# Loading the state of two batches first, and transposing the rest by DMA, in an attention and gated feed-forward kernel

## The chip, the cores and the metric

The kernel runs on one core of one Trainium2 chip. The metric is the device time of one execution in microseconds (us). TensorE does the products, ScalarE (ACT), VectorE (DVE) and GpSimd (POOL) the elementwise work, and the core has 16 DMA engines. Loads that GpSimd issues go through the "software" queue (q0 in the profile), loads and transposes that SyncE (SP) issues through the "hardware" queue (q1). Each run also records the clock granted to TensorE, as a share of full speed.

## The reference, cut to what matters

There are 8 batches, each with x (8 heads, 512 tokens, 64 wide) and a state (8 heads, 32 slots, 64 wide). Tokens attend to slots, slots attend to tokens, and everything goes through a gated feed-forward layer.

```python
scores = x @ state^T / 8;   xread = softmax(scores) @ state     # tokens read the state
scores2 = state @ x^T / 8;  sread = softmax(scores2) @ x        # slots read the tokens
y = concat(xread, sread)                                        # 4352 rows of 512
out = (sigmoid(y @ w_gate) * (y @ w_val)) @ w_out               # d_ff = 1536
```

## The kernel before

The kernel never forms xread. It multiplies the transposed state with the gate and value weights once per batch (SW, "gate states"), and the gate products are then the transposed attention weights (aT) times SW. Each batch so needs its x and its state transposed (xT, sTc) before its scores, and aT before its gate products. The first two batches are a hand-ordered list of steps (the "head"). The other batches are prepared one ahead, between the products of the batch before.

In the head, the whole state is loaded first, then x of batch 0 and 1 and the first 256 of the 1536 columns of the weights in f32, all on the hardware queue. TensorE transposes the whole state:

```python
sf = wp.tile((128, 16, D), FP, name="sf")
nc.sync.dma_start(sf, state.rearrange("b h (u l) d -> (b h u) l d", l=16))   # 4 KB a partition
load_x(0, nc.sync, 2)
...
for i in range(2):
    ps = p_gv.tile((128, 8, 64), FP, name="stp", tag="gv")
    for l in range(8):
        for e in range(2):
            nc.tensor.matmul(ps[e * 64:(e + 1) * 64, l], sb[:, 8 * i + l], ident_e[:, e], start=True, stop=True)
```

Later in the head, GpSimd issues the last weights, x of batch 2, w_out in three parts and x of batch 3. It then casts x of batch 2, and SP transposes it by DMA, four instructions a batch:

```python
load_x(2, nc.gpsimd)
load_wo(0); load_wo(1); load_wo(2)          # w_out
load_x(3, nc.gpsimd)
...
cast_x(2, pool, 0, 4); cast_x(2, pool, 4, 4)
cast_x(3, pool, 0, 4); cast_x(3, pool, 4, 4)
at_xT_dma(2); at_xT_dma(3)
```

After the head come the output products of batch 0 (12 groups of four), and between them the attention of batch 2 and its gate states:

```python
if b == 1 and f == 1:                       # after the second group of output products
    for i in range(2):
        S_mm(nb, i, (AT, OU)[i])            # scores of batch 2: TensorE, in order
        S_exp(nb, i); n_sum(nb, i); n_mul(nb, i, nc.vector)
    aT_dma(nb)                              # its attention weights, transposed by DMA
```

In the traces of this case an engine takes its instructions in program order, and what waits at the front holds up what stands behind it: in the changed kernel GpSimd stood for 15.0 us in front of one cast, with ready work behind it.

The softmax here doesn't subtract the row's maximum and nothing guards it: scores larger than these inputs give would overflow.

## Time and profile before

| | before |
|---|---|
| device time, median of the first 4 runs | 229.31 us (229.16 to 229.48) |
| profiled span, granted clock | 227.5 us, 1.0 |
| TensorE busy | 215.7 us (95%) |
| first output product of batch 0 starts | 44.89 us |
| scores of batch 2 start | 46.62 us |

The span is shorter than the device time, since it starts at the first instruction. TensorE is full from about 20 us to the end. The lines of the profile are in the prediction below.

### The profile page before, as it was taken

The numbers are of one execution on the slowest core, as the hardware profiler recorded it, in microseconds if no ns is written. First come the engines' busy times: TensorE is split into PE (matmuls) and PEld (weight loads), VectorE is DVE, ScalarE is ACT, GpSimd is POOL, SyncE is SP. The second block draws the span as 40 slices with busy tenths as digits, with TensorE's granted clock in tenths as the row PEclk, the third lists the DMA queues.
The fourth block names the chain that finished last, engine by engine and source line by source line (L and its number), as shares of the span: only waits on it lengthen the run. The fifth ranks groups of instructions, "written<-read, shape, count | busy, mean of one in ns | idle before, by whom it ended". The sixth has DMA issues, their size and how long they took to land.

```text
span 227.5 us, 4735 instructions
## 1 busy us (share of the span) xinstructions
PE 215.7 (95%) x1831; PEld 111.6 (49%) x1856; DVE 141.4 (62%) x234; ACT 131.0 (58%) x246; POOL 44.4 (20%) x78
## 2 busy tenths in 40 slices
PE   7568999999999999999999999999999999999994
PEld 7453345444454545444544454454445444466743
DVE  2599889967448855886488638874687433422301
ACT  3677877647476566746675666656755444423311
POOL 1499930060033001500060006000200000000001
PEclk9999999999999999999999999999999999999999
DMA  6999999943699252725282431243122111111113
GB/s 213 354 176 191 233 264 242 152 80 69 145 287 248 41 132 101 231 46 124 87 252 43 83 116 46 81 83 116 46 72 69 48 46 49 67 73 46 49 35 104
DMA packets 37990, 28.09 MB, mean 123 GB/s; under 512 B 20976, under 2 KB 33136, under 8 KB 37968
## 3 DMA queue, kind: packets, MB, share of 16 engines
q1 hardware_dynamic: 32464, 21.31, 35.3%
q0 software_dynamic: 5360, 6.42, 14.8%
q8 instruction: 14, 0.23, 0.4%
q14 instruction: 8, 0.07, 0.2%
q10 hardware_dynamic: 144, 0.07, 0.1%
HBM read 18.35 MB, written 8.91 MB: 120 GB/s over the span
## 4 chain that ended last, share of the span: by engine, by line
PE 76%; DMA 11%; POOL 5%; SPq 3%; issue 2%; ACT 1%; DVE 0%; POOLq 0%; ACTq 0%
PE outp L321 35%; PE gvp L290 28%; DMA xf<-in_x_dram 8%; PE gvp L293 5%; PE swp L238 4%; DMA xT<-xb 3%; SPq L128 2%; PE srp L215 1%; POOL Eb L145 1%; PE Sp L134 1%; PE outp L341 1%; POOL wg L83 1%; POOL ab L175 1%; POOL xb L103 1%; POOL wv L94 1%
## 5 line engine op out<-in xcount | busy, mean ns | idle before, releaser
L305 DVE SCALAR_TENSOR_TENSOR glu<-th,gvp 128x512 bf16<-128x512 f32 (+1 forms) x108 | 70.2, 657 | 63.9 <-ACT th L300 48.2
L300 ACT ACTIVATE th<-gvp 128x512 f32<-128x512 f32 (+1 forms) x108 | 61.6, 575 | 62.5 <-PE gvp L290 51.2
L290 PE MATMUL gvp<-aT,SW 128*128 128x512 bf16 x384 | 96.3, 379 | 0.2
L321 PE MATMUL outp<-wo,glu 128*128 128x512 bf16 x371 | 95.1, 379 | 1.3 <-issue 0.2
L290 PEld LDWEIGHTS <-SW 128*128 128x128 bf16 x384 | 36.2, 98 | 45.1 <-issue 4.2
L321 PEld LDWEIGHTS <-glu 128*128 128x128 bf16 x396 | 37.4, 98 | 40.7 <-issue 0.4
L276 ACT CAST SW<-swp 128x512 bf16<-128x512 f32 (+1 forms) x78 | 42.2, 582 | 4.2 <-PE swp L238 2.9
L145 POOL CAST Eb<-E 128x256 bf16<-128x256 f32 x32 | 12.4, 429 | 96.2 <-ACT E L139 96.2
L325 ACT ACTIVATE res<-outp 128x512 f32<-128x512 f32 x33 | 19.7, 598 | 17.1 <-PE outp L321 17.1
L103 POOL CAST xb<-xf 128x1024 bf16<-128x1024 f32 (+1 forms) x13 | 14.6, 1147 | 20.8 <-DMA xf<-in_x_dram 20.8
L276 DVE CAST SW<-swp 128x512 bf16<-128x512 f32 x20 | 13.4, 683 | 0.7 <-PE swp L238 0.7
L175 DVE TENSOR_TENSOR ab<-E,ri 128x512 bf16<-128x512 f32 x14 | 13.7, 980 | 0.1
L332 POOL DMA_DIRECT2D out_dram<-res x2 | 1.0, 526 | 60.1 <-ACT res L325 60.1
L160 DVE TENSOR_REDUCE E<-E 128x128 f32<-128x512 f32 x12 | 12.3, 1033 | 0.0
L152 DVE TENSOR_REDUCE rs<-E 128x16 f32<-128x512 f32 x16 | 10.8, 678 | 2.0 <-ACT E L139 2.0
L238 PE MATMUL swp<-wg,sTc 64*32 64x256 bf16 (+1 forms) x256 | 11.6, 328 | 0.3
L238 PEld LDWEIGHTS <-sTc 64*32 64x32 bf16 x512 | 6.4, 90 | 10.7 <-issue 7.9
L139 ACT ACTIVATE E<-Sp 128x512 f32<-128x512 f32 x16 | 9.6, 608 | 2.5 <-PE Sp L134 2.5
L238 PE MATMUL swp<-wv,sTc 64*32 64x256 bf16 (+1 forms) x256 | 10.3, 324 | 0.2 <-POOL wv L94 0.2
L220 DVE RECIPROCAL r<-srp 128x128 f32<-128x128 f32 x8 | 7.6, 951 | 1.5 <-PE srp L215 1.5
L134 PEld LDWEIGHTS <-xT 128*128 128x128 bf16 x128 | 5.7, 98 | 4.3 <-ACT xT L123 0.8
L134 PE MATMUL Sp<-sTz,xT 128*128 128x64 bf16 x128 | 6.4, 193 | 1.3 <-ACT xT L123 0.7
(54 smaller groups left out, 109.0 us busy)
## 6 DMA issues: line engine op xcount, KB each, us to landing
out_dram<-res SPq DMA_DIRECT2D x31, 256.0 KB, 2.5
xf<-in_x_dram SPq DMA_DIRECT2D x5, 1024.0 KB, 6.9
xf<-in_x_dram POOLq DMA_DIRECT2D x2, 1024.0 KB, 14.3
wo<-in_moe_w_out_dram POOLq DMA_DIRECT2D x3, 512.0 KB, 12.7
xf<-in_x_dram SPq DMA_DIRECT2D x2, 512.0 KB, 5.3
wg<-in_moe_w_gate_dram POOLq DMA_DIRECT2D x2, 512.0 KB, 7.1
wv<-in_moe_w_val_dram POOLq DMA_DIRECT2D x2, 512.0 KB, 7.7
sf<-in_state_dram SPq DMA_DIRECT2D x1, 512.0 KB, 3.7
```

The source lines that it names most:

```text
L103: cp(xbs[b].rearrange("p c h d -> p h c d")[:, lo:lo + n], xfs[b][:, lo:lo + n])
L134: nc.tensor.matmul(ps[:, c, :, jj], xTs[b][:, 2 * i + jj, c], sTz[:, b, 2 * i + jj], start=True, stop=True)
L145: nc.gpsimd.tensor_copy(Ebs[b][:, c], E1s[b][:, c])
L160: nc.vector.tensor_reduce(held["E4", b][:, e].rearrange("p j n -> p (j n)"), E1s[b][:, :, e].rearrange("p c j n -> p (j n) c"), AX.X, ALU.add)
L175: eng.tensor_tensor(abs_[b].rearrange("p c e (j n) -> p (c e) j n", n=Ns)[:, :, 2 * i:2 * i + 2], halfE(b, i), ri.unsqueeze(3).to_broadcas ...
L238: nc.tensor.matmul(pss[e][j * Ns:(j + 1) * Ns, o:o + n], sTc[rows, b, j], (wg, wv)[w][rows, j, lo:lo + n], start=True, stop=True)
L276: cp(*sw_left.pop((b, lo, w, e)))
L290: nc.tensor.matmul(ps, SWs[b][:, g, w, fs], aTs[b][:, :, g], start=(g == 0), stop=(g == 1))
L300: nc.scalar.activation(th, held["gv", b, f][0], AF.Tanh, scale=0.5)
L305: nc.vector.scalar_tensor_tensor(glus[b][:, f], held["th", b, f], 1.0, held["gv", b, f][1], ALU.add, ALU.mult)
L321: nc.tensor.matmul(ops[b, c], glus[b][:, f, c * 128:(c + 1) * 128], wo[:, f], start=(f == 0), stop=(f == NF - 1))
L325: nc.scalar.activation(res, ops[b, c], AF.Copy, scale=0.5)
```

## The change

The intent is to start sooner. Only the state of batches 0 and 1 (128 KB of 512 KB) is loaded at the start, behind x of batch 0. The state of batches 2 to 7 comes later and is transposed by DMA. The attention weights of batch 2, which DMA transposed, are transposed by TensorE. The first weights come by the software queue with a cast, and the steps of the head are in a new order.

```diff
-    sf = wp.tile((128, 16, D), FP, name="sf")
-    nc.sync.dma_start(sf, state.rearrange("b h (u l) d -> (b h u) l d", l=16))
-    load_x(0, nc.sync, 2)
+    load_x0(0)
+    load_x0(1)
+    nc.sync.dma_start(sf, state[0:2].rearrange("b h (u l) d -> (b h u) l d", l=4))
...
+    def load_sl():
+
+        nc.gpsimd.memset(sl[:, 0, 0, 0:1], 0.0)          # the gate: SP's loads wait for it
+        for j in range(4):
+            for e in range(2):
+                nc.sync.dma_start(sl[j * Ns:(j + 1) * Ns, :, e], state[2:B, 2 * j + e].rearrange("b n d -> n b d"))
+
+    def at_sT_dma(b):
+        nc.sync.dma_start_transpose(sTc[:, b].rearrange("p j n -> p (j n)"), slb[:, b - 2].rearrange("p e d -> p (e d)"))
...   (the head in a new order; weights of columns 0 to 255 by load_w in place of load_wf and cast_w)
     load_x(2, nc.gpsimd)
+    load_sl()
     load_wo(0)
...
-    pad(2, 6)
+    sl_cast(pool)
+    at_sT_dma(2)
     cast_x(2, pool, 0, 4)
     cast_x(2, pool, 4, 4)
+    at_xT_dma(2)
+    pad(2, pool)
+    at_sT_dma(3)
     cast_x(3, pool, 0, 4)
...
-                    aT_dma(nb)
+                if b == 1 and f == 5:
+                    aT_mm(nb, AT)
+                    aT_cp(nb, 0, vec)
+                    aT_cp(nb, 1, vec)
+                if b == 2 and f == 1:
+                    for q_ in range(4, B):
+                        at_sT_dma(q_)
+                    pad(4, pool, B - 4)
```

## The prediction

> **What bounds the kernel now.** I read the page first (shares and slices), then the windows view, the waits of TensorE, the chain of waits between 20 and 50 us, and the DMA queues in short windows.
>
> The page says that TensorE is the bound, except in the first 20 us. Each digit below is one fortieth of the span (5.7 us); the last row is the share of time in which the 16 DMA engines moved something.
>
> ```profile
> PE 215.7 (95%) x1831; PEld 111.6 (49%) x1856; DVE 141.4 (62%) x234; ACT 131.0 (58%) x246; POOL 44.4 (20%) x78
> PE   7568999999999999999999999999999999999994
> ...
> DMA  6999999943699252725282431243122111111113
> ```
>
> TensorE is at 5 to 7 tenths in the first three slices and full afterwards, so only there is time to be had: up to 20.29 us it was busy 13.46 us, of which 5.5 us (4.02, 0.83 and 0.62) were warm-up products. About 12.3 us of the first 20.3 did nothing useful. The second thing to see is the DMA row: it is full from about 5 us to about 45 us. The whole head is a race of loads as well.
>
> The waits of TensorE, summed, are all of the head:
>
> ```profile
> PE aTp L182 <- DVE ab L175: 2.1, 2, 1.1
> ...
> PE xTp L118 <- POOL xb L103: 1.0, 1, 1.0
> PE Sp L134 <- ACT xT L123: 0.7, 1, 0.7
> PE Sp L134 <- POOL sTz L391: 0.6, 1, 0.6
> PE xTp L118 <- DVE xb L103: 0.6, 1, 0.6
> ```
>
> They are links of the dependent chain of attention: x lands, cast, transpose, scores, exp, sum, product, transpose of the weights. The change attacks the beginning of this chain. But the chain of waits shows a second bound later (start us, duration us, what):
>
> ```profile
> 22.81 9.12 DMA xf<-in_x_dram
> ...
> 32.08 2.03 POOL xb L103 x2
> ...
> 36.77 2.93 SPq L128
> ...
> 39.74 7.14 DMA xT<-xb
> ...
> 46.93 0.33 PE Sp L134 x5
> ```
>
> The scores of batch 2 need x of batch 2, loaded at 22.81 and landed at 31.93, cast by GpSimd until 34.11, transposed by DMA. The transposes landed only at 46.88, and TensorE, in order, was just there (its first score product began at 46.62; it waited 0.2 us). So TensorE's arrival at this point and this chain of loads are level today. A faster head alone brings TensorE sooner to a place where it must wait.
>
> Why do transposes issued at 34.12 land at 46.88, when the group of issues gives a median of 2.5 us? In the window from 34.1 to 38 us (its row per queue is packets, MB, share of 16 engines) there is only the software queue, with the load of w_out; from 38 to 40 both queues move:
>
> ```profile
> q0 software_dynamic: 766, 0.78, 121.3%
> ```
> ```profile
> q0 software_dynamic: 216, 0.62, 98.4%
> q1 hardware_dynamic: 168, 0.04, 11.6%
> ```
>
> The hardware queue got nothing for almost 4 us, then roughly one packet for each packet of the software queue.
>
> **What the Trainium skill says.** "DMA: Bandwidth & Descriptors", section "Queues, rings and completion order": each DMA engine "round-robins between the queue rows it has work for, at *packet* granularity". The trace from 38 to 40 us agrees (168 against 216); that from 34 to 38 us is worse than that for the hardware queue (0 against 766). The same page, section "Specifications", gives 512 B as the least transfer at line rate; the new load of the later states has runs of 256 B (64 f32). No run yet shows those. "VectorE: DVE Perf Modes", "The three transpose paths", has 390 ns for a 128x128 transpose by TensorE and 1309 ns by DMA. Here eight TensorE transposes take 0.61 us in all (218 ns each, overlapped), a DMA transpose 1.24 to 1.27 us of issue; so aT of batch 2 costs TensorE about 0.45 us in a stream (0.61 less one product's latency of about 0.16), and saves four issues.
>
> **The change, part by part.**
>
> *Start.* Before: state (0.52 MB) landed at 4.42, the halves of x0 at 5.92 and 7.5, x1 at 10.51; each 0.52 MB takes 1.5 us. After: x0 halves at about 4.4 and 5.9, state of two batches (0.13 MB) at 6.3 to 6.5. The 24 state transposes that go save TensorE about 0.8 us, in a stretch where it idles anyway. Followed with the durations of the trace (cast of two heads 0.62 on ACT, 0.43 on DVE; eight transposes 0.62; exp 0.6; sum 0.68 plus 0.25): casts of heads 0 to 3 end at 5.0; state cast 6.5, its transpose 6.9, its copy 7.8, padding 8.1; the last copy of x's first half on DVE 8.5; first scores 8.6 to 9.0; first exp 9.05, against 9.87 before. So the earlier x gives 0.8 us, not 1.5, since the state is now the later link. The second exp stands behind the cast of x1's second half on ACT (1.05 us): x1 lands near 9.5 to 10.3, cast until 11.3, exp at 11.35 against 11.49. Most of the gain is gone there.
>
> *Middle of the head.* f32 staging and casts of the first weights (0.69 on DVE, 1.52 on GpSimd) go, and the software queue starts at about 6.7 instead of 12.8 us. But GpSimd gets Eb of batch 0 (1.9 us) ahead of the second product of batch 0 (1.06), so that product ends at about 16.8 and aT of batch 0 starts on TensorE at 16.9, against 15.55; its copy moves to ACT (1.0 instead of 0.63). The first gate products start at about 19.4, after which TensorE should not stop; before, that was 20.29. At 19.4 it has in addition done the state read of batch 0 (24 products, 0.9 us), but not aT of batch 1 (0.46) and one gate tile (0.87). So it is ahead by 20.29 - 19.4 - 0.43 = about 0.5 us. The eight transposes of batch 2 give 0.45 of that back later. My sum over the head is thus close to 0, give or take 1.2 us for links that I mis-sized.
>
> *The loads.* Bytes read up to and with x3 are the same: the state (0.52 MB) is split 0.13 + 0.39. The software queue starts 6 us sooner, but also carries 1 MB of weights that came by the hardware queue; at its rates (a 1 MB slice in 2.7 to 3 us) it would be done with the first two thirds of the weights at about 19, and waits for GpSimd to issue the last third (behind Eb of batch 1, which I put at 21). So x2 is issued at about 22.5 and lands at 30.5 to 32.
>
> *State of batches 2 to 7.* 8 loads of 192 runs of 256 B, 1536 packets or 96 on each engine, issued after x2. GpSimd in order then waits for them, casts them (about 0.8 us), and only then casts x2 (2.03 us); SP issues one more transpose (about 1.3 us) ahead of x2's four. With loads that land with x2: transposes of x2 issued from 34 to 39.5, behind w_out as today, landing at 46.5 to 47.5, +0 to +1 us. With strict alternation at one packet each (80 ns for a weight packet plus some 45 ns): 96 turns are about 10 us or more, the states land near 39 to 41, x2 is cast until 43, transposes land near 49 to 50, and TensorE waits 3 us or so.
>
> Attention of batch 2 then runs from scores to product in about 4.1 us (47.34 to 51.39 before); the TensorE transposes sit after four output groups of 0.86 us and the gate states' 0.84: no wait, or a small one. Before, aT's DMA transposes were issued from 53.59 to 58.6 and landed just ahead of 59.9, where TensorE wanted them, so this part removes a risk, not time.
>
> **Rivals.** (1) *The head gains, and nothing takes it back.* If I mis-sized the head by 1 to 2 us and x2's transposes come sooner too, since the software queue is ahead by up to 2 us: 226.5 to 228. For it: idle and warm-up of 12 us in the head; against it: x2's chain is level with TensorE now. (2) *The new wait for the late states takes over*: 232 to 234. For it: 256 B packets against a full software queue, GpSimd waiting in order, the 0 packets in 4 us seen above. Against it: the queue may take several packets of a DMA at a turn, and the loads stand behind a gate placed with care. (3) *x1 is starved* by weights now free to start at 6.7 us (before, a gate held them until x1 landed): x1 at 12.8 instead of 10, as one packet each would make it, head 2 us longer, total 231 to 232. Against it: x1's descriptors are queued first. (4) *Hidden*: DMA total sets the scores of batch 2 in both, 229 to 230.
>
> **Range and chances.** Rival 4 with its +0 to +1 us of x2's chain, mixed with 1, is the middle: 229.4 + 0.45 (transposes) + about 0.5 (later scores) - about 0.6 (chance of a better head). That gives 229.7. Rival 1 at its best sets the low end, rival 2 the high one: 226.5 to 233.6. Faster by over 2% (under 224.8) needs more than 4.6 us, over a third of the head's loss, with x2 4 us earlier: 0.06. Slower by over 2% (over 234.0) needs a wait of over 4 us: 0.13.
>
> **What would show it.** In the new profile: first exp near 9.0 and second near 11.4; x1 landed by 10.3; the first aT transpose on TensorE near 16.9; TensorE without a gap after about 19.4; x2 landed at 30.5 to 32; a wait of TensorE for x2's transposes near 46 of 0 to 3 us, and GpSimd's cast of the late states before 35 (or after 39 in rival 2). The prediction is wrong if the scores of batch 2 run before 45 us, or if x1's cast or the late states' landing is the longest wait of the head.

## The result, and the profile after

The changed kernel took 236.6 us (median of 4 runs, 235.64 to 237.7) against 229.31 us. It is slower by 3.2%: the ratio is 1.0319, with a 95% interval of 1.0269 to 1.0369. Ratios here are the mean time of one kernel's runs over that of the other's of the same rounds, so they are not quite the ratios of the medians. Executions over 1.5% slower than the fastest of the same kernel are left out of the means.

The page of the changed kernel, with the granted clock:

```profile
span 233.8 us, 4758 instructions
...
PE 221.0 (95%) x1844; PEld 114.0 (49%) x1844; DVE 139.3 (60%) x237; ACT 130.4 (56%) x244; POOL 46.5 (20%) x86
...
PE   7689999839999999999999999999999999999994
...
PEclk9889999988999999999999999999999999999999
DMA  6996999746834525543444351135112111112113
```

The third slice of TensorE went from 6 to 8, so the head looks denser (a part of this is the half clock in that slice, at which the same products are busy for longer). But there is a hole in the eighth slice (41 to 47 us, an 8, with the worse part in the ninth, a 3), and the clock row, all 9 before, has 8s in the second and third slice and again in the hole's second half and behind it.

The waits of TensorE name the hole. It waits three times for transposes of x, and before that for the padded state (sTz):

```profile
PE Sp L134 <- DMA xT<-xb: 3.7, 3, 2.0
...
PE Sp L134 <- POOL sTz L412: 1.1, 1, 1.1
...
PE swp L238 <- DVE aT L192: 0.5, 1, 0.5
```

The chain of waits between 22 and 54 us of the changed kernel shows where these come from (start us, duration us, what):

```profile
22.01 0.90 POOL xf L78
...
26.70 14.05 DMA sl<-in_state_dram
...
41.88 2.04 POOL xb L103 x2
...
48.32 2.50 DMA xT<-xb
...
50.86 0.87 PE Sp L134 x13
```

The load of x of batch 2, issued at 22.0, landed after 10.5 us, at 32.5. This landing is not in the chain: that of the late states (sl) is. They were issued from 23.05 us on and landed at 40.8 to 41.0. GpSimd stood in front of their cast for 15.0 us, with x of batch 2 ready behind it. Then come cast, cast of x, transposes, scores, each step as late.

Why the states took so long, the DMA queues show in the window from 32 to 39 us (packets, MB, share of the 16 engines):

```profile
q0 software_dynamic: 1102, 1.10, 92.2%
q1 hardware_dynamic: 1100, 0.26, 29.6%
```

On average one packet of the states moved for each packet of w_out: 1100 against 1102. The states' packets carry 256 B, those of w_out 1 KB, so the states got a fifth of the bytes. They have 1536 packets, 96 for each engine, and needed as many turns. "DMA: Bandwidth & Descriptors", section "Queues, rings and completion order", of the Trainium skill describes such turns, and the trace agrees in the counts. Two things add to this. None of the states' packets moved before 27.1 us, 4 us after the first issue. And the software queue paid too: it moved 157 packets a us beside the states (1102 in 7 us), against 196 alone in the kernel before (766 in 3.9 us).

After the wait, TensorE ran at half clock (windows view; the last three numbers are clock, share of DMA, GB/s):

```profile
50.00:52.00 2.00, 1.14 (x15) 0.86 (x16) 0.00 (x0) 0.59 (x2) 0.00 (x0) 0.71 0.20 40
52.00:54.00 2.00, 2.00 (x20) 0.57 (x26) 1.83 (x4) 0.49 (x2) 1.83 (x5) 0.50 0.56 112
```

The clock record of the trace has this stretch from 50.86 to 54.27 us, 3.41 us long, and another one in the head, from 9.9 to 13.3 us. The Trainium skill says of this, in "TensorE: Matmul & The Clock Gate", "Part 1: The HAM clock gate", that TensorE falls to half rate after about one idle window of some 3.4 us. The trace agrees behind the wait: TensorE was busy 0.41 us from 47.44 to 50.86, and the half-clock stretch has that length. (The head is another matter, see "What stays open".) The four output products at 51.55 took 1.89 us against 1.03 us for the same four at 47.32 before.

The timelines of TensorE give a sum. First before, then after (start, duration, engine, line, operation):

```profile
44.89 1.89 PE L321 MATMUL outp<-wo,glu 128*128 128x512 bf16 x7
46.62 0.86 PE L134 MATMUL Sp<-sTz,xT 128*128 128x64 bf16 x16
47.32 1.03 PE L321 MATMUL outp<-wo,glu 128*128 128x512 bf16 x4
```
```profile
43.59 1.89 PE L321 MATMUL outp<-wo,glu 128*128 128x512 bf16 x8
...
51.55 1.89 PE L321 MATMUL outp<-wo,glu 128*128 128x512 bf16 x4
...
54.56 2.76 PE L321 MATMUL outp<-wo,glu 128*128 128x512 bf16 x12
```

| stretch of TensorE's work | before, us | after, us | after minus before |
|---|---|---|---|
| start to first output product of batch 0 | 44.89 | 43.59 | -1.30 |
| to the end of the scores of batch 2 | 2.43 | 7.96 | +5.53 |
| to the end of the first gate states of batch 2 | 2.16 (to 49.48) | 3.01 (to 54.56) | +0.85 |
| to the end of its second gate states | 3.67 (to 53.15) | 4.83 (to 59.39) | +1.16 |
| the rest | 174.4 | 174.5 | +0.1 |
| span | 227.5 | 233.8 | +6.3 |

So the head did gain 1.3 us. The scores of batch 2 cost 5.5 us, the half clock behind them 0.85, and the stretch with the TensorE transposes of aT 1.16. The half clock began with the last 13 score products, so a little of the 5.5 us is its own (0.30 us, see e4).

### The profile page after: what moved, and what is told of

It is laid out like the page before. It is cut to its first block, busy times and chain, and to the rows that moved or that the text cites. A ratio compares the mean times of both kernels' runs of the same rounds, so it can differ in the third digit from the quotient of the medians.

```text
span 233.8 us, 4758 instructions
## 1 busy us (share of the span) xinstructions
PE 221.0 (95%) x1844; PEld 114.0 (49%) x1844; DVE 139.3 (60%) x237; ACT 130.4 (56%) x244; POOL 46.5 (20%) x86
## 4 chain that ended last, share of the span: by engine, by line
PE 78%; DMA 9%; SPq 4%; POOL 3%; DVE 2%; ACT 2%; issue 1%; POOLq 0%; DVEq 0%
PE outp L321 36%; PE gvp L290 27%; DMA sl<-in_state_dram 6%; PE gvp L293 4%; PE swp L238 4%; DMA sf<-in_state_dram 2%; SPq L128 2%; PE Sp L134 2%; SPq L401 1%; PE srp L215 1%; PE outp L341 1%; DMA xT<-xb 1%; POOL xb L103 1%; POOL ab L175 1%; PE warm L355 1%
## 5 line engine op out<-in xcount | busy, mean ns | idle before, releaser
L321 PE MATMUL outp<-wo,glu 128*128 128x512 bf16 x396 | 98.9, 382 | 0.0
L321 PEld LDWEIGHTS <-glu 128*128 128x128 bf16 x396 | 37.6, 98 | 41.1 <-issue 1.0
L276 ACT CAST SW<-swp 128x512 bf16<-128x512 f32 x75 | 41.8, 586 | 4.6 <-PE swp L238 3.3
L152 DVE TENSOR_REDUCE rs<-E 128x16 f32<-128x512 f32 x16 | 10.9, 680 | 9.0 <-ACT E L139 9.0
L276 DVE CAST SW<-swp 128x512 bf16<-128x512 f32 x21 | 14.1, 681 | 0.7 <-PE swp L238 0.7
L134 PE MATMUL Sp<-sTz,xT 128*128 128x64 bf16 x128 | 7.3, 202 | 6.1 <-DMA xT<-xb 3.7
L134 PEld LDWEIGHTS <-xT 128*128 128x128 bf16 x128 | 6.2, 103 | 9.7 <-DMA xT<-xb 5.6
L238 PE MATMUL swp<-wv,sTc 64*32 64x256 bf16 (+1 forms) x256 | 10.5, 331 | 0.0
L175 DVE TENSOR_TENSOR ab<-E,ri 128x512 bf16<-128x512 f32 x12 | 10.3, 858 | 0.1
```

Of the source, the lines that this page charges most:

```text
L134: nc.tensor.matmul(ps[:, c, :, jj], xTs[b][:, 2 * i + jj, c], sTz[:, b, 2 * i + jj], start=True, stop=True)
L175: eng.tensor_tensor(abs_[b].rearrange("p c e (j n) -> p (c e) j n", n=Ns)[:, :, 2 * i:2 * i + 2], halfE(b, i), ri.unsqueeze(3).to_broadcas ...
L238: nc.tensor.matmul(pss[e][j * Ns:(j + 1) * Ns, o:o + n], sTc[rows, b, j], (wg, wv)[w][rows, j, lo:lo + n], start=True, stop=True)
L276: cp(*sw_left.pop((b, lo, w, e)))
L321: nc.tensor.matmul(ops[b, c], glus[b][:, f, c * 128:(c + 1) * 128], wo[:, f], start=(f == 0), stop=(f == NF - 1))
```

## The experiments

The theory: GpSimd, in order, waits for late states that crawl, because each of their small packets takes its turn against a large one (A). The half clock is a second part of the loss (D), and the TensorE transposes of aT a third (E). The rivals: the small packets slow all traffic and the order is of no matter (B), the hardware queue is shut out altogether (A2), the clock is of no matter. Twelve runs of kernels (two are repeats) were made, in four sessions on three chips, each beside runs of the kernel before. Unless a base is named, the edit is to the changed kernel. The kernel before took 229.59 to 233.91 us in the first session (7 runs, one slow), 229.09 to 231.37 in the second and third (12 runs), and 228.89 to 230.5 in the fourth (11 runs). Some of its runs now had half-clock stretches too (clock 0.984 to 0.993), of which the first four, from 229.16 to 229.48, give no sign. So I compare times by ratio within a session, and rest more on places in the trace than on times.

### e1_x2_first: cast x of batch 2 ahead of the late states

```diff
-    sl_cast(pool)
-    at_sT_dma(2)
     cast_x(2, pool, 0, 4)
     cast_x(2, pool, 4, 4)
     at_xT_dma(2)
+    sl_cast(pool)
+    at_sT_dma(2)
     pad(2, pool)
```

> Edit: GpSimd casts x of batch 2, and SP issues its four transposes, before the cast and the transpose of the late states; nothing else moves. Theory A (GpSimd waits in order for the late states, which land at 41.0 in the changed kernel, and x of batch 2, there since 32.5, waits behind them): x2 is cast near 32.5 to 34.6, its transposes share the queue behind what is left of the state loads and land near 45 to 46.5; the state of batch 2 is cast at 41, transposed behind them, padded near 47; TensorE waits 2 to 3 us before the scores of batch 2 instead of 5.4 in all, and the total is 233.0 to 234.5. Rival B (the 1536 small packets slow all loads, order is of no matter): x2 itself and its transposes come no sooner, 236 or more.

Measured: 233.43 us (232.23 to 234.76), ratio 1.0117 (1.0037 to 1.0196). x was cast at 32.89 and no longer waited for. What TensorE waited for at the scores is now the padded state alone (waits of TensorE: who, for whom, us in total, times, longest):

```profile
PE Sp L134 <- POOL sTz L412: 3.0, 1, 3.0
```

The wait fell from 4.8 us in four pieces to 3.0 us, as A has it, and the state of batch 2 was padded only at 48.1. (The 5.4 us in the expectation count 0.6 us of a score product in the head as well.) So the order on GpSimd is a part of the loss. What is left comes from the late landing (cast at 40.86), since the padded state is made from it, and no order on GpSimd mends that.

### e2_sl_early: issue the late states ten microseconds sooner

```diff
+    load_sl()
     gate(xfs[1][:, 0, 0, 0:1])
...
     load_x(2, nc.gpsimd)
-    load_sl()
     load_wo(0)
```

> Edit: the gate (memset) and the eight loads of the late states move up on GpSimd's queue, from behind the load of x of batch 2 (22.9 us) to ahead of the third gate (near 13.1 us), so that they can use the gap of the software queue at 19.5 to 22.5 us. Theory A: they land before 25 us, x of batch 2 is cast as soon as it lands (31 to 33), the scores of batch 2 run near 46 with a wait under 1 us, TensorE's clock stays up in that stretch, total 227.5 to 229.5. Rival C (the small packets alternate with weight packets instead and weights come late): TensorE stalls for weights of the second third near 22 to 24 us by 1 to 3 us, total 230 to 232.

Measured: 229.63 us (229.37, 229.59, 229.67 and once 232.44), ratio 0.9991 (0.9885 to 1.0097). The states were issued from 12.4 us on and were all there before 24.9, when GpSimd came to cast them without a wait. The price feared under C was small: TensorE waited 0.18 us for weights at 22.48. The first output product came at 42.94, 1.95 us ahead of before, and the scores of batch 2 were done at 46.35 (timeline of TensorE; in brackets the wait before a line and what ended it):

```profile
42.94 1.89 PE L321 MATMUL outp<-wo,glu 128*128 128x512 bf16 x8
44.67 0.52 PE L134 MATMUL Sp<-sTz,xT 128*128 128x64 bf16 x2
45.49 0.20 PE L134 MATMUL Sp<-sTz,xT 128*128 128x64 bf16 x1 [0.30 <-DMA xT<-xb]
45.96 0.55 PE L134 MATMUL Sp<-sTz,xT 128*128 128x64 bf16 x13 [0.27 <-DMA xT<-xb]
46.35 1.03 PE L321 MATMUL outp<-wo,glu 128*128 128x512 bf16 x4
```

One moved line takes the loss away within the noise, so the late landing of the states is shown as its main cause; the next run tests why they were late. But nothing is gained over the kernel before, though the head is 1.95 us shorter. The next runs ask where those went. The lines above name one place: the transposes of x of batch 2 land where they did before, near 46, and the stretch from the first output product to the end of the scores is 3.41 us instead of 2.43. So 0.98 us stay there.

### e3_sl_3kb: the same bytes in 128 long runs

```diff
-        for j in range(4):
-            for e in range(2):
-                nc.sync.dma_start(sl[j * Ns:(j + 1) * Ns, :, e], state[2:B, 2 * j + e].rearrange("b n d -> n b d"))
+        flat = state[2:B].rearrange("b h n d -> (b h n d)")
+        nc.sync.dma_start(sl.rearrange("p b e d -> p (b e d)"), flat.rearrange("(p k) -> p k", p=128))
```

> Edit: the late states are loaded by one DMA with 3 KB runs (128 runs in place of 1536 of 256 B), same bytes, same place; the data lands in the wrong order, so the result is wrong on purpose. Theory A1 (queues alternate packet by packet, so 96 packets an engine need 96 turns): 8 turns are enough, the states land before 30 us, and the kernel shows what the rest of the change is worth: 227.5 to 229.5. Rival A2 (the hardware queue gets nothing while weight loads that cast are queued): the states land after 38 us and the total stays at 235 to 237.

Measured: 231.66 us (230.94 to 232.09), ratio 1.0036, and the result is wrong as meant (the states are in the wrong order). The states, issued at 22.2 as late as in the change, landed 6.6 us later and were cast at 28.92, not at 41 (their cast in the view by tile: ns, first and last start, form):

```profile
L403 POOL CAST slb<-sl x1: 822/822/822, 28.9 to 28.9; 128x768 bf16<-128x768 f32 x1
```

That is A1, and A2 falls: it is the number of packets, not the queue as such. (One instruction also took the place of eight, but that did not start the load sooner: its first packet moved at 25.8 us, again 3.6 us after the issue.) The total missed what I expected by 1.4 us and more. x of batch 2 was cast at 32.45, 1.1 us later than in the run before, its transposes landed later still, and TensorE waited 2.0 us for them. Why x came later is not shown.

### e4_filled: keep TensorE busy through the wait

```diff
                 if b == 1 and f == 1:
+                    warm(70, SWP)
                     for i in range(2):
```

> Edit: 70 warm-up products (128x128x128, 55 ns each at full clock, 3.9 us) just before the scores of batch 2, where TensorE waits anyway until 50.9 us. Theory D (a part of the loss is the half clock that TensorE is granted from 50.9 to 54.3 us after idling): the wait ends at the same time, the clock stays full there, and the total falls by 1 to 2 us to 234.5 to 235.5, with less spread between runs. Rival (the half clock costs nothing, the wait is all): 236 to 237 as before.

Measured: 233.84 us (233.33 to 235.26), ratio 1.0143, with clock 1.0 in three of four runs. In the stretch where the clock had been halved (windows view, clock third from the end):

```profile
50.00:52.00 2.00, 1.86 (x41) 1.05 (x49) 0.94 (x2) 1.15 (x3) 0.65 (x3) 1.00 0.38 77
52.00:54.00 2.00, 2.00 (x33) 0.84 (x17) 1.83 (x5) 1.50 (x3) 1.82 (x4) 1.00 0.36 70
```

The stretch from the scores to the end of the first gate states is 1.94 us (50.30 to 52.24), against 3.01 in the change and 2.16 before. So the half clock is worth about 1.1 us here, and D holds: a filled wait is cheaper than an idle one. Another 0.30 us lie in the last 13 score products, whose start is 0.39 us ahead of the next output product here and 0.69 in the change. That makes 1.37 us for one stretch. The head of this profile had no half-clock stretch either, which an edit 30 us later does not explain, and its scores ended at 50.30, sooner than the 51.55 of the change. So the difference of the totals is not all due to the edit.

### e5_aT_dma: aT of batch 2 by DMA again

On the kernel of e2:

```diff
                         n_mul(nb, i, nc.vector)
-                if b == 1 and f == 5:
-                    aT_mm(nb, AT)
-                    aT_cp(nb, 0, vec)
-                    aT_cp(nb, 1, vec)
+                    aT_dma(nb)
```

> Edit on the kernel with the late states loaded early (the second run): the attention weights of batch 2 are transposed by four DMA transposes again, as before the change. Theory E (the TensorE transposes cost 0.46 us of work and 0.53 us of a wait, since the next gate states need the PSUM tile that they leave to two copies on DVE; the DMA ones would still be in time): 0.5 to 1.0 us less than that kernel, 228.5 to 229. Rival F (TensorE now gets there 2 us sooner, and the DMA transposes, behind the four of x of batch 3 on SP, land late): TensorE waits 1 us or more before the gate products of batch 2, total 229.5 to 231.

Measured: 230.2 us (229.21 to 231.39), ratio 1.0008 (0.9968 to 1.0048). The stretch with the second gate states took 3.89 us (51.06 to 54.95) instead of 4.83 in e2, so 0.94 us are back as E has it. Then TensorE waited 0.40 us ahead of the first gate product of batch 2. The profile puts that down to a copy of ACT, and whether the DMA transposes were the later of its two inputs was not settled (the last was issued at 59.7 and landed about 2.4 us later, the product began at 62.19). The time cannot tell 0.5 us here, and this profile's head was 2.2 us late for another reason (it waited 2.9 us for the first state's cast). In time this run is inconclusive.

### e6_aT_swp: another PSUM tile for these transposes

On the kernel of e2:

```diff
-                    aT_mm(nb, AT)
+                    aT_mm(nb, SWP)
```

> Edit on the kernel with the late states loaded early: the TensorE transposes of batch 2 go to a PSUM tile of the four that the gate states use last, not to the one that they use first. Theory E: the wait of 0.53 us of a gate product for the copy of aT goes, total 0.4 to 0.6 us less than with the other tile, 228.8 to 229.3. Rival: the wait moves to another tile and nothing is gained, 229.4 to 229.8.

Measured: 230.19 us (228.78 to 231.69), ratio 1.0005 (0.9955 to 1.0056). Three runs at a clock of 0.999 or more took 228.78 to 229.29. The others, at 0.985 to 0.993, took 231.1 to 231.69. In the trace the wait for the copy of aT fell, as expected (waits of TensorE):

```profile
PE swp L238 <- DVE aT L192: 0.2, 1, 0.2
```

and the stretch is 4.40 us (48.43 to 52.83) instead of 4.83. The gain of 0.4 us is seen in the trace, while the time does not resolve it.

### e7_before_aT_pe: this part of the change alone, on the kernel before

```diff
                         n_mul(nb, i, nc.vector)
-                    aT_dma(nb)
+                if b == 1 and f == 5:
+                    aT_mm(nb, AT)
+                    aT_cp(nb, 0, vec)
+                    aT_cp(nb, 1, vec)
```

> Edit on the kernel before: only the attention weights of batch 2 are transposed by TensorE as in the change. Theory E: the change's third part alone costs TensorE 0.46 us of work and about 0.5 us of wait: 0.5 to 1.0 us slower than before (ratio 1.002 to 1.005). Rival: the DMA transposes bound something in the kernel before, and it is no slower or faster (ratio 1.000 or less).

Measured: 230.46 us (229.82 to 231.49), ratio 1.0011 (0.9971 to 1.0051). The sign and size are E's, but the interval holds 1. The trace has the same stretch as in the change, 4.83 us (50.73 to 55.56) against 3.67 before, with the same 0.53 us of wait. The 1.16 us in the table are thus this part's.

### e8_changed_again: the changed kernel, unedited

> The changed kernel, unedited, on the chip of these runs. If the half clock after the long wait belongs to the kernel, it shows in each run again: mean clock under 0.995 always, total 235 to 238. If it was that chip's or that moment's, the clock is 1.0 in some runs and those take about 234.

Measured: 234.42 us (234.04 to 235.32), ratio 1.0192 (1.0157 to 1.0228). The clock was below 0.995 in all six runs (0.983 to 0.993), as in the first four (0.976 to 0.985). One stretch of 3.41 us at half clock is 0.007 of the mean clock, so by their mean clock the runs of the first chip had two or three of them, and those of this one one or two. The loss is 1.9% here and 3.2% there; that the clock makes this difference is not shown. In this profile the half clock ran from 48.2 to 55.1 us. Half clock began at the end of the wait in every profile in which TensorE waited 3 us or more there (the change, e1, e8 and e9). In the runs without a profile a low mean clock may also come from the head.

### e9_wo_later: two thirds of w_out behind the cast of x of batch 2

On the kernel of e6:

```diff
     load_wo(0)
-    load_wo(1)
-    load_wo(2)
-    load_x(3, nc.gpsimd)
...
     cast_x(2, pool, 4, 4)
+    load_wo(1)
+    load_wo(2)
+    load_x(3, nc.gpsimd)
```

> Edit on the kernel with the late states early and aT of batch 2 in another PSUM tile (the sixth run): GpSimd casts x of batch 2 before it issues the second and third load of w_out and the load of x of batch 3, so that the DMA transposes of batch 2 do not stand behind three loads of w_out and one of x. Theory G (these transposes, landing near 46, are what takes back the head's gain; by themselves they would take some 5 us from 33.5): they land before 43, TensorE's wait of 0.6 us before the scores of batch 2 and the loose products there (about 1 us in all) go, total 0.5 to 1.2 us less than the sixth run's kernel in the same rounds, and under the kernel before by 0.3 to 0.6%. Rival H (w_out is then late for the output products, or x of batch 3 for the scores of batch 3): TensorE waits there 1 us or more and nothing is gained or 1 to 2 us lost.

Measured: 233.95 us (232.66 to 235.44), ratio 1.0181 (1.0135 to 1.0227). This was a clear miss: the transposes landed at 48.6, later than before, and TensorE waited 3.4 us for them. Neither theory had that. From 36 to 43 us, by queue:

```profile
q0 software_dynamic: 1028, 1.07, 91.5%
q1 hardware_dynamic: 918, 0.23, 29.1%
```

The transposes of one batch are about 2048 packets of 256 B. Beside loads they take about as many turns as the loads do, like the late states (918 against 1028). I had issued the loads at 33.7 us, together with the transposes, so that all of these ran beside traffic.

### e10_aT_swp_again: e6 once more, beside e9

> The sixth run's kernel unedited, on the chip of the ninth, to compare with it in the same rounds: by theory G 0.5 to 1.2 us slower than the ninth run's kernel, within 0.3% of the kernel before.

Measured: 230.6 us (228.5 to 232.91), ratio 0.998 (0.9922 to 1.0038). Runs at a clock of 0.998 or more took 228.5 to 229.32, those at 0.984 to 0.993 took 231.89 to 232.91, two of them slow. The intervals of e9 and this run do not meet, so e9's loss is the edit's.

### e11_wo_gated: the last third of w_out and x of batch 3 wait for the transposes

On the kernel of e6:

```diff
     load_wo(1)
-    load_wo(2)
-    load_x(3, nc.gpsimd)
...
     at_xT_dma(2)
     pad(2, pool)
+    gate(xTs[2][:, 3, 3, 0:1])
+    load_wo(2)
+    load_x(3, nc.gpsimd)
```

> Edit on the sixth run's kernel: the third load of w_out and the load of x of batch 3 are issued only when the last transpose of x of batch 2 has landed (GpSimd reads one element of it). The ninth run showed that the 2048 small packets of these transposes alternate with weight packets one to one. Theory G2: with only the second load of w_out beside them they land near 42 to 43, before TensorE comes (44.7), the waits there go, and the total is 0.5 to 1.2 us under the sixth run's kernel: 228.0 to 228.6 in runs at clock 1.0. Rival H: the last third of w_out lands after 48 and TensorE waits for it by 1 us or more: 229.5 to 231.

Measured: 228.08 us (227.6 to 230.02), ratio 0.9942 (0.9903 to 0.9982). The transposes landed at 41.8, and the scores ran without a wait (timeline of TensorE):

```profile
42.95 1.89 PE L321 MATMUL outp<-wo,glu 128*128 128x512 bf16 x7
44.68 0.63 PE L134 MATMUL Sp<-sTz,xT 128*128 128x64 bf16 x16
45.15 1.03 PE L321 MATMUL outp<-wo,glu 128*128 128x512 bf16 x4
```

The interval lies below 1, so this version beats the kernel before, by 0.6%, and it is correct. (By the rule that asks for 2% the verdict is "same". The changed kernel was not run beside it, and the lead over it is that of the ratios.) Nor was the kernel of e6: that the gate gains on e6 is seen in the trace alone, where the scores ended at 45.15 instead of 46.49. The version keeps the new head and leaves the small packets only the second load of w_out beside them, whose last packet moved at 36.8 us.

### e12_both_gated: the second third of w_out behind the gate as well

On the kernel of e11:

```diff
-    load_wo(1)
...
     gate(xTs[2][:, 3, 3, 0:1])
+    load_wo(1)
     load_wo(2)
```

> As the run before, with the second load of w_out behind the same gate too. Theory G2: the transposes are alone, land near 41, but the second third of w_out lands only near 46, where TensorE needs it: a wait of 0 to 1 us, 228 to 229.5 at clock 1.0. Rival H: it lands after 47 and costs 2 us or more: 230 to 231.5.

Measured: 231.2 us (230.93 to 234.01), ratio 1.0086 (1.0044 to 1.0128). The transposes landed at 40.9. The scores had no wait, but TensorE waited twice for w_out (waits of TensorE):

```profile
PE outp L321 <- DMA wo<-in_moe_w_out_dram: 1.4, 2, 0.7
```

The wait of 1.4 us lies between what the two theories gave, the total is that of H: the gate may hold one third of w_out, not two. The profile's head was also 1.1 us later than that of e11.

## Why the prediction was wrong

I predicted 229.7 us within 226.5 to 233.6 and gave a slowdown of over 2% a chance of 0.13. The kernel took 236.6 us. The mechanism was among the rivals, complete with its places in time. I chose another one as the middle.

**The step that failed** is in the paragraph on the state of batches 2 to 7 together with the range: "Rival 4 with its +0 to +1 us of x2's chain, mixed with 1, is the middle". In its place stood rival 2. Its steps, predicted and measured: the states land near 39 to 41 (40.8 to 41.0), x of batch 2 is cast until 43 (43.9), its transposes land near 49 to 50 (50.8). By the prediction's own signs this was rival 2 (the cast of the late states after 39: 41.1), and its last sign of being wrong, the landing of the late states as the longest wait, came true as well: 15.0 us on GpSimd. The evidence was at hand, in the view that the prediction itself shows: 168 hardware packets beside 216 of the software queue. Against it I set the hope that the queue takes several packets at a turn. No view showed such a thing, and e2 and e3 show that the count of packets decides.

**Terms of the sum that were mis-sized or missing.** Rival 2 was put at 232 to 234, and the profile's run took 235.64. Three terms make up the difference:

- The wait: "TensorE waits 3 us or so". The stretch grew by 5.53 us, since TensorE came 1.3 us sooner (43.59) and the transposes a little later.
- The clock: no step of the prediction had it. It cost 0.85 us behind the scores in the table (1.07 by e4) and 0.30 us in the scores themselves, and by their mean clock the three other runs of the change had about one stretch more than the profiled one.
- The transposes of aT: "about 0.45 us in a stream", "no wait, or a small one". They cost 1.16 us. The missing part is 0.53 us of waiting for the PSUM tile that the two copies on DVE hold, the rest the work itself. e6 takes about 0.4 us of it away by another tile.

**The head.** Predicted ahead by about 0.5 us, it was ahead by 1.30 us with a half-clock stretch in it, and by 1.95 us without (e2). My first links were too early (first exp at 9.05 predicted, 10.13 measured; second 11.35, 12.27), the middle ones too late: Eb of batch 0 took 1.42 us on GpSimd instead of 1.9, aT of batch 0 began at 15.74 instead of 16.9, and the first gate product at 17.81 instead of 19.4. The sign was right. That the early and the late errors pulled in opposite directions was luck. And rival 3 (x1 starved) did not happen: x1 landed at 10.9, and the software queue moved almost nothing before 9 us.

**What was right.** "A faster head alone brings TensorE sooner to a place where it must wait" is what e2 shows once the late states are out of the way: 1.95 us gained in the head, 0.98 lost again at the scores and 1.16 at the aT transposes. That leaves an end level with the kernel before. e11 shows the first of these losses directly. With the transposes landed at 41.8, the stretch to the end of the scores is 2.20 us, and the time falls below that of both kernels.

**What stays open.** The profile does not settle whether aT of batch 2 by DMA would still be in time in e11 (e5 had a wait of 0.4 us of mixed cause).

Turns do not explain the whole of the transposes' delay, neither in the prediction's reading nor here. In the kernel before, from 44 to 45 us, the hardware queue moved 261 packets and the software queue none, yet the transposes landed only at 46.88; in the next us the hardware queue moved 682. Why it was slow with nothing beside it, no run asked.

Why the head gets a half-clock stretch in some runs and not in others was not tested, but the traces narrow it. The clock changes only on a grid of 3.41 us. In the twelve profiles that show the grid there are 12 windows of it in which TensorE was busy for 1.77 us or less, about half (busy time as the windows view has it). After 11 of them the clock was halved (the change: 1.72 us busy from 6.49 to 9.90; e10: 1.70 from 46.06 to 49.48), and after no window with more. The head lies on this edge: its window has 1.78 us in the kernel before (full clock) and 1.72 in e7 (halved). So a wait need not be long to cost clock. The clock is not all of the spread, though: the kernel before took 229.09 us at a mean clock of 0.992 and 231.32 at 0.999.

## What to carry to other kernels

Before a load moves, count its packets, not only its bytes: beside a queue of large packets, a load of n small ones on each engine needs about n turns, so put it where the other queue is empty, or give it long runs. Before a queue in order gets a new wait, ask what stands behind it, since here x of batch 2 was ready for 9 us behind a cast that it did not need. And when a change brings an engine sooner to its next wait, look for what sets that wait first, and add the clock to the price of idling.

## What the Trainium skill lacked or had wrong

- "DMA: Bandwidth & Descriptors", "Queues, rings and completion order": the rule of turns is right, and the page says that a packet is typically 9 to 17 descriptors. Here as many recorded packets of 256 B moved as of 1 KB (1100 against 1102 in 7 us). Whether a recorded packet is the page's packet or one of its descriptors, the trace does not say. The page does not say what follows for a load in short runs: the 0.39 MB of late states took until 41.0 us from an issue at 23.05 to 27.2, and 6.6 us in 3 KB runs.
- The same page: a newcomer to busy engines waits before it gets its first turn. The states, issued from 23.05, had no packet between 23 and 27 us, while the software queue moved 756. The transposes issued at 34.12 before had none until 38. In e12 and e11, where no load or one was queued ahead, the first packet of the transposes moved 1.2 and 1.3 us after the issue. I found this delay of about 4 us on no page, and its cause is open.
- "DMA Transpose (X-bar)" on that page does not say what a transpose costs beside other loads. Four transposes issued at about 34 us landed at 40.9 alone (e12), at 41.8 with one load of w_out beside them at first (e11), at 46.9 behind two loads of w_out and one of x (before), and at 48.6 with the same three started alongside (e9).
- "TensorE: Matmul & The Clock Gate" has the half clock after an idle window of some 3.4 us. Here windows in which TensorE was busy for half of the time (1.70 us of 3.42 in e10) were followed by it too. In "Terms" the page prices it as the throttled time times (1 - K/N), by which a stretch of 3.41 us at half clock would cost an estimated 1.7 us; measured were 1.37 us in the change against e4, and 1.37 in e10 against e6.
- "VectorE: DVE Perf Modes", "The three transpose paths", compares TensorE's 390 ns with DMA's 1309 ns. It says that this path ends in PSUM, but not what it costs that the tile is held until a copy is done: eight transposes cost TensorE 1.16 us in the kernel, 0.53 of it waiting for the tile.
